# A gated mix of memory attention and a Fourier filter: fewer, larger numerator loads, split transposing loads, and a new order

## The chip, the core and the metric

One core of a Trainium2 chip runs the whole program. Its engines work side by side and in order, each through its own list of instructions: PE (TensorE, matrix products into PSUM), DVE (VectorE), ACT (ScalarE) and POOL (GpSimd) for elementwise work, and SP (SyncE), which here issues nearly all DMAs. PEld is the weight load of PE. The metric is the time of one execution on the device in microseconds, as the median of several runs.

## The reference

The input x has 2,048 tokens of 640 numbers. The result is a gate per token between two branches over the same x:

```python
g = sigmoid((x * gate_w).sum(-1, keepdims=True))
a = A(x, wq, wk, wv, wo, beta)
b = irfft2(rfft2(x) * (w_r + 1j * w_i))          # over tokens and channels
return g * a + (1 - g) * b
```

Branch A is attention in 4 segments of 512 tokens with 32 heads of 20 numbers. Inside a segment it is causal attention with softmax. Beside that, each head keeps a memory matrix M (20 x 20) and a sum z over all earlier segments:

```python
p = softmax(qs @ ks.T * scale + mask);  a_dot = p @ vs
a_mem = (phi(qs) @ M) / (phi(qs) @ z + 1e-6)
o = sigmoid(beta) * a_mem + (1 - sigmoid(beta)) * a_dot
M += phi(ks).T @ vs;  z += phi(ks).sum()
```

The o of all segments goes through wo. In segment 0 the memory is empty, so only a_dot counts.

## The kernel before

**Recording and replaying.** The program is not emitted in the order in which it is written. `record` (line 687 on) calls the parts one after another, and each operation is stored with what it reads and writes. `schedule` (line 104) then takes a list of numbers, PLAN (line 431 on), and emits in its order: a number divided by 16 is the operation, half of it modulo 8 is the engine, and its lowest bit picks for some PE products whether they run as one product of 128 columns or as four of 32. A second list gives the PSUM bank of each accumulation. So PLAN sets both the order on each engine and the choice of engine where there is one (`either`: DVE or POOL, `copy`: ACT or DVE). `emit` (line 140) puts in the waits that the dependences need. Nothing else decides the order; on each engine a late operation holds all behind it.

**Attention.** For a segment, `project` makes q, k and v from x, which transposing loads have turned. `attend` (line 1083 on) makes scores in PSUM, ACT exponentiates them (L1229, L1225), POOL or DVE set the masked part to zero (L1255, L1254), and `pv` multiplies with v. v carries a column of ones, so that each head's product has its numerators and, beside them, its denominator. The result is evicted (tile ub) and stored, tokens along the row, to a scratch tensor in HBM, u_scr: a segment has 1,024 rows of 512 tokens, 32 rows to a head, of which 20 are numerators and one the denominator.

**Denominators.** `denominators` loads the denominators of a segment back, takes reciprocals, multiplies by the gates and stores them to r_scr. From there each segment's r4 tile is loaded so that a partition holds the reciprocals of the head that it works for. Segment 3 has no time for that round trip: its reciprocals are built on PE (`pair_inverse`, `inverse_table`), for the first 24 heads (LATE) in r4, and for the last 8 heads separately (`late_group`, tile oL).

**Memory.** `mem_read_tile` (line 1032 on) multiplies phi(q) of 128 tokens with the masked memory matrix into two PSUM banks, computes the gated reciprocals of the denominators (tile dn), and one DVE product (name mem_mul, L1061 for segments 1 and 2, L1072 for segment 3) writes the quotients, tokens on the partitions, to the tile mem. The place of an element in a row of mem is chosen so that the row can be used turned: it is stored to HBM (o_scr; for segment 3 another scratch tensor with 6 x 128 columns), and later a transposing load brings it back as mT, channels on the partitions.

**Finishing.** `finish_tile` works on 128 tokens of a segment (a = 0 to 3). For a = 0 it loads the numerators of the whole segment as chunks of a tile oU: chunk c has 512 tokens in the row, and its partition (head, j) holds dimension 4c + j (segments 0 to 2: 5 chunks, 32 heads x 4) or 5c + j (segment 3: 4 chunks, 24 heads x 5). Each chunk is loaded alone (L1412, ld_u) and multiplied in place by r4 (L1414, normal). For a = 0 and 2 the memory part of 256 tokens is fetched by a transposing load (L1424, oT) into one of two mT buffers, with 5 or, in segment 3, 6 blocks of 128 channels. For each a, L1427 adds mT to oU (addmem); in segment 3, L1432 adds blocks 4 and 5 to oL (addlate). Then PE sums, in one PSUM bank per half row, the Fourier part (weights from the gate table) and the chunks times matching rows of wo (`late_weights` loads those, L772 and L777), and the row is evicted and stored.

The Fourier branch (`fft`) runs on the same engines beside the attention of all segments.

Of the kernel before, what the change touches and what calls it, by code (L numbers as in the profile page):

```python
# [8 lines left out]
ALU = mybir.AluOpType  # L9
# [3 lines left out]
P = 128  # L13
# [337 lines left out]
class Kern:  # L351
# [65 lines left out]
    def dma(self, dst, src, nbytes, r, w, tr=False, name="", after=(), queues=("sp",)):  # L417
# [1074 lines left out]
```

## Time and profile before

| what | value |
|---|---|
| time, median of 3 runs | 243.28 us (242.96 to 243.37) |
| the profiled execution | 241.93 us, its span 240.2 us |
| granted TensorE clock | 0.999 |
| PE busy | 220.6 us, 92% of the span |
| DVE busy | 209.2 us, 87% |
| ACT busy | 198.7 us, 83% |
| POOL busy | 134.2 us, 56% |
| DMA, mean | 183 GB/s |

The profile is of one execution. A row of a group of instructions names the line in the program, the engine, the operation, the tile written and the tiles read with their shapes, the number of instructions, then the busy time in us and the mean duration of one in ns, and at last the engine's idle time in front of them with what ended it. PE matrix products overlap, so a PE that is busy is not a PE at its peak. The tile mT shows under its own name, o_scr is the HBM tensor that it is loaded from, r is r4.

### The profile page before, as it was taken

The page shows a single profiled execution, that of the slowest core. Times are in us where ns is not written, and L with a number is a line of the kernel's source. Part 1 is how long each engine was busy: PE and PEld are TensorE (multiplying, and loading weights), DVE is VectorE, ACT ScalarE, POOL GpSimd, SP SyncE. Part 2 cuts the span into 40 slices and gives each one's busy share as a digit, 9 for nine tenths or more (in the row PEclk, how much of TensorE's full clock was granted, in tenths as well). Part 3 has the DMA queues.
Part 4 walks back from the last instruction along what each step waited for, and adds up shares of the span by engine and source line. Part 5 has one row for each costly group of instructions (what it writes and reads, how often), then busy time and mean ns, then how long its engine had stood idle before and what let it go on. Part 6 is the DMA issues. An engine that isn't in the chain of part 4 may idle for free.

```text
span 240.2 us, 9491 instructions
## 1 busy us (share of the span) xinstructions
PE 220.6 (92%) x4004; PEld 138.0 (57%) x4018; DVE 209.2 (87%) x476; ACT 198.7 (83%) x226; POOL 134.2 (56%) x205
## 2 busy tenths in 40 slices
PE   6989979999999889999998999999978999799994
PEld 2865546665654547555755457656544555466673
DVE  0889979999999899999999989899999996867752
ACT  2489879999999988988999799997989598589321
POOL 8613154547647594676659563694686606753100
PEclk9999999999999999999999999999999999999999
DMA  7999979989959764269769847565875899594323
GB/s 196 317 242 271 235 221 154 296 217 166 233 153 206 177 179 142 68 185 176 236 183 200 182 113 232 167 184 178 200 174 167 177 214 120 114 191 129 109 104 113
DMA packets 61897, 43.92 MB, mean 183 GB/s; under 512 B 31232, under 2 KB 58656, under 8 KB 61856
## 3 DMA queue, kind: packets, MB, share of 16 engines
q1 hardware_dynamic: 60816, 42.76, 76.0%
q8 instruction: 31, 0.51, 0.9%
q10 hardware_dynamic: 1040, 0.57, 0.8%
q14 instruction: 10, 0.08, 0.1%
HBM read 23.42 MB, written 13.87 MB: 155 GB/s over the span
## 4 chain that ended last, share of the span: by engine, by line
PE 43%; DVE 32%; ACT 8%; POOL 6%; issue 5%; DMA 3%; SPq 2%; DVEq 0%; POOLq 0%
PE psum L401 39%; ACT ex L1229 5%; POOL exc L1255 4%; DVE Pt L1346 4%; PE psum L399 4%; DVE G L1388 3%; DVE ub L408 2%; DVE Yt L1351 2%; DMA x<-in_A_x_dram 2%; DVE va L408 2%; SPq L423 2%; DVE Ac L408 2%; DVE mem L1072 2%; ACT exc L1225 2%; DVE Bt L408 1%
## 5 line engine op out<-in xcount | busy, mean ns | idle before, releaser
L1229 ACT ACTIVATE ex<-psum 128x2048 bf16<-128x2048 f32 x64 | 120.2, 1878 | 12.8 <-PE psum L401 12.1
L1255 POOL TENSOR_SCALAR_AFFINE_SELECT ex<-ex 128x256 bf16<-128x256 bf16 (+2 forms) x93 | 54.5, 593 | 49.7 <-ACT ex L1229 34.9
L1255 POOL TENSOR_SCALAR_AFFINE_SELECT exc<-exc 128x512 bf16<-128x512 bf16 (+3 forms) x23 | 29.1, 1271 | 10.4 <-DVE exc L1254 7.3
L401 PE MATMUL psum<-qkp 20*64 20x64 bf16 (+5 forms) x1024 | 31.1, 266 | 3.4 <-DMA qkp<-qk_scr 1.3
L401 PE MATMUL psum<-xT,wk 128*128 128x256 bf16 (+1 forms) x276 | 29.7, 273 | 0.5 <-issue 0.5
L401 PE MATMUL psum<-xT,wq 128*32 128x256 bf16 (+1 forms) x161 | 25.1, 326 | 1.2 <-issue 1.0
L1346 DVE TENSOR_TENSOR Pt<-psum,Wt 128x642 bf16<-128x642 f32 x32 | 25.7, 821 | 0.3 <-PE psum L401 0.2
L401 PE MATMUL psum<-wv,xT 128*32 128x320 bf16 (+3 forms) x387 | 24.5, 300 | 0.4 <-DVE Pt L1346 0.4
L401 PEld LDWEIGHTS psum<-qkp 20*64 20x64 bf16 (+1 forms) x1024 | 12.6, 100 | 19.1 <-ACT ex L1229 8.6
L401 PEld LDWEIGHTS psum<-xT,wk 128*128 128x128 bf16 (+1 forms) x276 | 19.9, 97 | 5.2 <-issue 2.0
L401 PE MATMUL psum<-ex,va 128*32 128x384 bf16 (+2 forms) x384 | 20.4, 320 | 1.9 <-POOL ex L1255 0.7
L401 PE MATMUL psum<-wo,oU 128*128 128x320 bf16 (+1 forms) x114 | 18.6, 300 | 0.0
L836 POOL TENSOR_TENSOR xsb<-xf 128x320 bf16<-128x320 bf16 (+2 forms) x12 | 9.0, 750 | 16.7 <-DVE xsb L836 13.7
L401 PEld LDWEIGHTS psum<-wv,xT 128*32 128x32 bf16 (+1 forms) x387 | 13.8, 96 | 6.4 <-issue 1.1
L408 DVE CAST ub<-psum 128x512 bf16<-128x512 f32 x23 | 15.7, 683 | 1.9 <-PE psum L401 1.4
L408 ACT ACTIVATE ot<-psum 128x320 bf16<-128x320 f32 x21 | 8.7, 440 | 10.5 <-PE psum L399 4.2
L1225 ACT ACTIVATE exc<-psum 128x1024 bf16<-128x1024 f32 (+1 forms) x12 | 15.7, 1308 | 1.8 <-PE psum L401 1.4
L1388 DVE TENSOR_TENSOR G<-eo,psum 128x320 bf16<-128x320 f32 x32 | 14.9, 481 | 1.8 <-ACT eo L408 1.4
L401 PE MATMUL psum<-big,Ac 128*128 128x161 bf16 (+2 forms) x93 | 14.2, 258 | 0.7 <-DVE mem L1061 0.3
L1254 DVE TENSOR_TENSOR ex<-ex,mk 128x256 bf16<-128x256 bf16 (+2 forms) x35 | 13.7, 397 | 1.0 <-ACT ex L1229 0.9
L401 PEld LDWEIGHTS psum<-xT,wq 128*128 128x128 bf16 (+1 forms) x175 | 10.4, 97 | 7.2 <-issue 0.7
L401 PEld LDWEIGHTS psum<-ex,va 128*32 128x32 bf16 x384 | 8.0, 95 | 11.2 <-issue 2.7
(145 smaller groups left out, 459.5 us busy)
## 6 DMA issues: line engine op xcount, KB each, us to landing
qkp<-qk_scr SPq DMA_DIRECT2D x28, 160.0 KB
tt<-tab_tt SPq DMA_DIRECT2D x8, 512.0 KB, 4.2
u_scr<-ub SPq DMA_DIRECT2D x15, 256.0 KB, 3.9
qk_scr<-qu SPq DMA_DIRECT2D x12, 256.0 KB, 2.1
xsb<-in_A_x_dram SPq DMA_DIRECT2D x8, 320.0 KB, 4.9
oU<-u_scr SPq DMA_DIRECT2D x15, 128.0 KB, 2.6
out_dram<-ot SPq DMA_DIRECT2D x12, 160.0 KB
Wt<-in_B_w_r_dram SPq DMA_DIRECT2D x16, 80.2 KB, 4.1
```

The source lines that it names most:

```text
L399: h = e.matmul(dst, wt, r_, start=st, stop=sp_, **{**kw, "tile_position": (0, q), "skip_group_check": True})
L401: h = e.matmul(o_, l_, r_, start=st, stop=sp_, **({**kw, "skip_group_check": True} if mode < 0 else kw))
L408: fns = {"act": lambda e: e.activation(dst(), src(), ACT.Copy), "dve": lambda e: e.tensor_copy(dst(), src())}
L423: return e.dma_start(d_, s_)
L836: self.either(lambda e, dst=dst, src=src, d0=d0, n=n, op=op: e.tensor_tensor(xs.ap(o + dst, [D, 2], [1, n]), xf.ap(src + d0, [321, 2], [1, ...
L1072: self.one("dve", lambda e, q0=q0, n=n, d0=d0, dst=dst, src=src, bc=bc: e.tensor_tensor(self.mem.ap(o + d0, *dst), self.ps(bank, q0 * VW, ...
L1225: self.one("act", lambda e, i=i: e.activation(self.exc.ap(self.exco(s, g + i), [192, 4], [768, m], [1, 128]), self.ps(bank, 128 * i, [512, ...
L1229: self.one("act", lambda e: e.activation(self.ex.ap(*d), self.ps(bank, *q), ACT.Exp, scale=SC), n, [bank], [self.exb(s, 2 * pr + gp, ks + ...
L1254: fns = {"dve": lambda e: e.tensor_tensor(av(d0), av(s0), mk(), ALU.min), "pool": lambda e: e.affine_select(ap(d0), ap(s0), [[0, 4 * m], [ ...
L1255: "pool": lambda e: e.affine_select(ap(d0), ap(s0), [[0, 4 * m], [step, n // 64], [1, 64]], ALU.is_ge, 0.0, base=base, channel_multiplier=-1)}
L1346: self.one("dve", lambda e, ri=ri, Pt=Pt, Wt=Wt, wo_=wo_, bank=bank: e.tensor_tensor(Pt.ap(ri * 322, [644, 2], [1, KD]), self.ps(bank, 0, ...
L1388: self.one("dve", lambda e, q=q, n2=n2, bank=bank, eo=eo: e.tensor_tensor(self.G.ap(n2 * D + 639 * q, [1 - 2 * q, 320]), eo.ap(q, [1, 320] ...
```

## The change

Four things change together.

1. The chunks of oU hold other dimensions: partition (head, j) of chunk c now has dimension 5j + c (segments 0 to 2) or 4j + c (segment 3). So neighbouring chunks of a partition are neighbouring rows of u_scr, and one descriptor can bring several. Chunks are loaded three and two at a time (segment 3: two and two), and each load is followed by one product over all its chunks, with r4 repeated. The loads of wo take the rows in the new order.
2. The memory products write the quotients to the places that the new chunks need. The number of elements and of instructions is the same; the loops over the chunks and over j change places, in the PSUM source and in the destination.
3. In segment 3 the transposing load of 6 blocks becomes two: blocks 4 and 5 first (with a dependence of its own, mL, which addlate waits for), and blocks 0 to 3 (mT, which addmem waits for).
4. PLAN is replaced as a whole: 2,223 operations instead of 2,243, with another order on every engine, other choices of engine and other PSUM banks. ACT issues the first load of wk, SP that of wq, which was the other way round.

```diff
-            self.dma(lambda c=c: self.wo[c].ap(0, [1, D]), lambda c=c: dap(self.wo_d, 4 * c * D, [DH * D, H], [D, 4], [1, D]),
+            self.dma(lambda c=c: self.wo[c].ap(0, [1, D]), lambda c=c: dap(self.wo_d, c * D, [DH * D, H], [5 * D, 4], [1, D]),
...
-            self.dma(lambda c=c: self.wo3[c].ap(0, [1, D], np_=5 * nh), lambda c=c: dap(self.wo_d, 5 * c * D, [DH * D, nh], [D, 5], [1, D]),
+            self.dma(lambda c=c: self.wo3[c].ap(0, [1, D], np_=5 * nh), lambda c=c: dap(self.wo_d, c * D, [DH * D, nh], [4 * D, 5], [1, D]),
...
             self.one("dve", lambda e: e.tensor_tensor(
-                self.mem.ap(i * D, [64, 2], [4, 16], [P, 5], [1, 4]), self.ps(bank, 0, [512, 2], [VW, 16], [4, 5], [1, 4]),
-                dn.ap(32, [16, 2], [1, 16], [0, 5], [0, 4]), ALU.mult), 640, [bank, rb], self.memb(s, i),
+                self.mem.ap(i * D, [64, 2], [4, 16], [1, 4], [P, 5]), self.ps(bank, 0, [512, 2], [VW, 16], [5, 4], [1, 5]),
+                dn.ap(32, [16, 2], [1, 16], [0, 4], [0, 5]), ALU.mult), 640, [bank, rb], self.memb(s, i),
...
-                (0, nh, 0, ([5 * nh, 2], [5, nh], [P, 4], [1, 5]), ([512, 2], [VW, nh], [5, 4], [1, 5]), ([0, DH],)),
+                (0, nh, 0, ([5 * nh, 2], [5, nh], [1, 5], [P, 4]), ([512, 2], [VW, nh], [4, 5], [1, 4]), ([0, DH],)),
...
-            for c in range(nc_):
-                home = (self.after_mid(("oU", c)) if s == 0 else [b("phq", t) for t in range(5)] if s == 1 else
+            for c0, n in ((0, 3), (3, 2)) if s < 3 else ((0, 2), (2, 2)):
+                home = (self.after_mid(("oU", c0)) if s == 0 else [b("phq", t) for t in range(5)] if s == 1 else
                         [b("va", 0, lt) for lt in range(4)] if s == 2 else [b("wqa"), b("wqb")])
-                self.dma(lambda c=c: oT.ap(c * L, [1, L], np_=np_), lambda c=c: dap(self.ud.ap(), (s * 1024 + nd * c) * L, [32 * L, nh], [L, nd], [1, L]),
-                         np_ * L * 2, [b("ud", s, i) for i in range(ng)], [ob[c]], name="ld_u", after=home)
-                self.either(lambda e, c=c: e.tensor_tensor(oT.ap(c * L, [1, L], np_=np_), oT.ap(c * L, [1, L], np_=np_),
-                                                           self.r4[s].ap(0, [1, L], np_=np_), ALU.mult), L, [b("r4", s)], [ob[c]], name="normal")
+                self.dma(lambda c0=c0, n=n: oT.ap(c0 * L, [1, n * L], np_=np_),
+                         lambda c0=c0, n=n: dap(self.ud.ap(), (s * 1024 + c0) * L, [32 * L, nh], [nc_ * L, nd], [1, n * L]),
+                         np_ * L * 2 * n, [b("ud", s, i) for i in range(ng)], ob[c0:c0 + n], name="ld_u", after=home)
+                self.either(lambda e, c0=c0, n=n: e.tensor_tensor(
+                    oT.ap(c0 * L, [L, n], [1, L], np_=np_), oT.ap(c0 * L, [L, n], [1, L], np_=np_), self.r4[s].ap(0, [0, n], [1, L], np_=np_), ALU.mult),
+                    n * L, [b("r4", s)], ob[c0:c0 + n], name="normal")
...
-                src = (lambda: dap(self.od.ap(), (s * L + a * P) * D, [D, 2 * P], [1, D])) if s < 3 else (
-                    lambda: dap(self.o3d.ap(), a * P * 6 * P, [6 * P, 2 * P], [1, 6 * P]))
-                self.dma(lambda mT=self.mT[k2]: mT.ap(0, [2 * P, n], [1, 2 * P]), src, 2 * P * P * n * 2,
-                         [b("od", s, i) for i in range(4)], [b("mT", k2)], tr=True, name="oT", after=self.after_mid(("mT", k2)))
+                src = (lambda k0: dap(self.od.ap(), (s * L + a * P) * D, [D, 2 * P], [1, D])) if s < 3 else (
+                    lambda k0: dap(self.o3d.ap(), a * P * 6 * P + k0 * P, [6 * P, 2 * P], [1, 2 * P + 2 * P * (k0 == 0)]))
+                for k0, m, key in ((0, 5, "mT"),) if s < 3 else ((4, 2, "mL"), (0, 4, "mT")):
+                    self.dma(lambda mT=self.mT[k2], k0=k0, m=m: mT.ap(k0 * 2 * P, [2 * P, m], [1, 2 * P]), lambda k0=k0: src(k0), 2 * P * P * m * 2,
+                             [b("od", s, i) for i in range(4)], [b(key, k2)], tr=True, name="oT", after=self.after_mid(("mT", k2)) + [b("mT", k2)])
...
-                                                                 mT.ap((4 + gl) * 2 * P + m0, [1, P]), ALU.add), P, [mb], [b("oL", gl, a)], name="addlate")
+                                                                 mT.ap((4 + gl) * 2 * P + m0, [1, P]), ALU.add), P, [b("mL", self.mtk[s])], [b("oL", gl, a)], name="addlate")
```

233 rows, old and new, of the table PLAN are left out of this document.

## The prediction, made before the changed kernel ran

> **What bounds the kernel now.** I read the page first (busy shares, the chain that ended last), then the busy times by stretch, then the waits of each stretch. The stretches: 76 to 146 us is the attention of segment 1, most of segment 2's and the middle of the Fourier branch; 146 to 184 the rest of segment 2 and the start of segment 3; 184 to 208 the last of the Fourier branch beside the first output tiles; 208 to 237 the output projections.
>
> ```profile
> PE 220.6 (92%) x4004; PEld 138.0 (57%) x4018; DVE 209.2 (87%) x476; ACT 198.7 (83%) x226; POOL 134.2 (56%) x205
> PE 43%; DVE 32%; ACT 8%; POOL 6%; issue 5%; DMA 3%; SPq 2%; DVEq 0%; POOLq 0%
> ```
> ```profile
> 76.00:146.00 70.00, 66.32 (x1174) 40.97 (x1180) 67.20 (x137) 64.74 (x63) 47.14 (x74) 1.00 0.70 169
> 146.00:184.00 38.00, 34.60 (x594) 21.13 (x593) 35.79 (x83) 34.28 (x38) 25.38 (x40) 1.00 0.68 189
> 184.00:208.00 24.00, 21.38 (x428) 12.43 (x428) 20.69 (x47) 19.19 (x24) 12.55 (x13) 1.00 0.83 151
> 208.00:237.00 29.00, 28.82 (x586) 19.14 (x586) 19.74 (x58) 16.21 (x23) 9.04 (x13) 1.00 0.59 134
> ```
> The columns are the stretch, its length, then busy time of PE, PEld, DVE, ACT and POOL, the granted clock (full speed here), the DMA share and GB/s. From 76 to 184 PE and DVE both work almost without a hole (PE idles 3.7 and 3.4 us, DVE 2.8 and 2.2), so more work on DVE there has little room. From 208 on PE never stops, DVE idles 9.3 us: the end comes when PE has done its matmuls, and it moves by what PE was held up before. The chain of waits from 171 to 179 us runs on DVE, through the memory read-out of the last segment:
>
> ```profile
> 171.61 0.72 DVE mem L1072
> 174.12 0.71 DVE mem L1072
> 176.92 0.71 DVE mem L1072
> 178.47 0.70 DVE mem L1072
> ```
> PE waits for just these products. The rows give total, times and longest; the first is from 76 to 146, the second from 146 to 184:
>
> ```profile
> PEld psum L401 <- DVE mem L1061: 1.8, 2, 1.2
> ...
> PEld psum L401 <- DVE mem L1072: 1.3, 3, 0.6
> ```
>
> **The change, part by part.** *Loads and normalisations of the numerators.* 19 loads become 8, 19 products become 8.
>
> ```profile
> L1414 DVE TENSOR_TENSOR oU<-oU,r 128x512 bf16<-128x512 bf16 x8 | 3.1, 413 | 0.0
> L1414 DVE TENSOR_TENSOR oU<-oU,r 120x512 bf16<-120x512 bf16 x3 | 1.1, 417 | 0.0
> L1414 POOL TENSOR_TENSOR oU<-oU,r 128x512 bf16<-128x512 bf16 x7 | 8.0, 1155 | 1.1 <-DMA r<-r_scr 0.7 <-DMA oU<-u_scr 0.4
> L1432 DVE TENSOR_TENSOR oL<-oL,mT 128x128 bf16<-128x128 bf16 x7 | 1.3, 219 | 0.0
> L1254 DVE TENSOR_TENSOR exc<-exc,mk 128x1024 bf16<-128x1024 bf16 x4 | 2.8, 690 | 0.7 <-POOL exc L1255 0.6
> ```
> On DVE (413 - 219) / 384 = 0.505 ns per element and 0.154 us fixed, so 1,024 elements take 0.67 us, which the mask product of that size (0.69, also with a repeated operand) confirms, and 1,536 take 0.93. The plan's numbers, decoded, put segment 0 on POOL and the other three on DVE: 2 x (0.93 + 0.67) + 2 x 0.67 = 4.5 us against 8 x 0.413 + 3 x 0.417 = 4.6. So DVE wins nothing here: it saves five fixed costs and takes over two products. POOL goes from 8 products (9.2 us) to two; by bounds of 1,155 ns per 512 elements (no fixed cost) these take at most 5.8, so it saves at least 3.4, on an engine that is 56% busy. I count that as nothing.
>
> The queue:
>
> ```profile
> L423 SPq DMA_DIRECT2D oU<-u_scr x19: 516/602/1560, 165.8 to 221.1; - x19
> DMA to landing us min/median/max: 2.5/2.6/3.2
> L421 SPq DMA_TRANSPOSE mT<-o_scr x6: 1342/1725/3625, 170.4 to 209.7; - x6
> DMA to landing us min/median/max: 7.3/7.7/8.1
> L421 SPq DMA_TRANSPOSE xT<-in_A_x_dram x9: 1241/1292/3195, 4.2 to 110.9; - x9
> ```
> SP issues 11 loads less (11 x 0.60 = 6.6 us) and two transposing loads more. A small transposing load (xT) still takes 1.29 us to issue, so the split costs 2.6 at that price, and the queue is 4.0 us lighter. What it would free is late next: after 184 us the transposes wait for their buffer and for landed data, not for the queue. A 384 KB load lands later than a 128 KB one (2.6); doubling that as an estimate, 2.6 us more, falls before products that wait on the reciprocals anyway. In the last segment the plan issues the split pairs where the two whole ones stood (206.9 and 209.7 us); both have landed by about 221 (209.7 + 3.6 + 8.1), and their first reader starts at 225.9. The four u loads that follow, at 218.3, become two, which gives back the 2.6. I take 0 for all DMA edits, bounds -1 and +1 us.
>
> *The memory products write another way.* This follows from the new row order (chunk c now holds dimensions 5j+c) and adds no instruction. Before, each product wrote runs of 4 or 5 neighbours; now consecutive elements lie 128 apart, 256 bytes.
>
> ```profile
> L1061 DVE TENSOR_TENSOR mem<-psum,dn 128x640 bf16<-128x640 f32 x8 | 6.6, 825 | 0.4
> L1072 DVE TENSOR_TENSOR mem<-psum,dn 128x480 bf16<-128x480 f32 x4 | 2.8, 706 | 0.1
> L1072 DVE TENSOR_TENSOR mem<-psum,dn 128x160 bf16<-128x160 f32 x4 | 1.3, 320 | 0.1
> L929 DVE COPY gT<-psum 8x128 f32<-8x128 f32 x4 | 1.5, 372 | 0.0
> L408 DVE COPY eo<-psum 128x321 f32<-128x321 f32 x4 | 1.9, 483 | 0.1
> ```
> No row shows a 256-byte step, so it is bounded. Lower end: runs of 4 cost nothing visible, since 160 elements take 320 and 640 take 825, or 1.05 ns per element throughout; +0. The other end: the gT copy is the one DVE instruction of this trace that writes every element away from its neighbour (32 bytes). Scaling the eo copy of the same type gives 483 - 193 x 1.05 = 280 ns for 128 elements; it takes 372, so 0.72 ns more per element. The 480 form supports it: 320 + 320 x 1.05 = 656 by the slope, 706 measured, where runs of 5 straddle. At 0.72 a 640 product takes 825 + 460 = 1.29 us; a 480 product 656 + 345 = 1.00, 0.30 more than now. 8 x 0.46 + 4 x 0.30 = +4.9 us of DVE. I take this end, since gT is nearest in kind (every write alone); both ends stay in the range. The Trainium skill (Advanced Engine Details and Errata, SBUF Cachelines) says that SBUF has 16-byte lines and that an access pattern which goes to a new line each time pays; the gT row (0.72 ns per element) agrees, and by a rule without price the sum would only be above the lower end.
>
> *The new order.* Decoded, the lists hold the same 1,082 PE operations; they reorder neighbours (no PE operation moves more than 21 places), and 201 changes of tile mode become 204. A weight load held by such a change shows as issue:
>
> ```profile
> PEld psum L401 <- issue: 6.2, 24, 0.5
> ```
> That is 0.26 us each, so 3 more cost 0 (hidden) to 0.8; I take 0.3. Between engines some work moves:
>
> ```profile
> L1254 DVE TENSOR_TENSOR ex<-ex,mk 128x256 bf16<-128x256 bf16 x20 | 7.2, 368 | 0.1
> L1254 DVE TENSOR_TENSOR exc<-exc,mk 128x512 bf16<-128x512 bf16 x8 | 4.0, 511 | 0.6 <-ACT exc L1225 0.6
> L408 DVE CAST Cp<-psum 128x512 bf16<-128x512 f32 x12 | 8.1, 682 | 0.2 <-PE psum L401 0.2
> L408 DVE CAST ot<-psum 128x320 bf16<-128x320 f32 x11 | 5.3, 485 | 5.7 <-PE psum L399 3.0 <-PE psum L401 2.6
> L836 DVE TENSOR_TENSOR xsb<-xf 128x320 bf16<-128x320 bf16 x9 | 2.8, 326 | 0.7 <-POOL xsb L836 0.7
> ```
> DVE gives 7 masks net to POOL (at 0.37 to 0.51, 2.6 to 3.6) and 3 late additions (0.22 each, 0.7). It takes 3 evictions net (0.49 to 0.68, 1.5 to 2.0, less the longer ones it gives away: about 1.1) and 3 folds and Fourier additions (0.33 each, 1.0). With the rows' lower ends that is -2.6 - 0.7 + 1.1 + 1.0 = -1.2. Summed along the decoded order, about 0.9 of it is gained by segment 2's last memory product (143 us) and 1.4 by 184 us. ACT saves 1.0 (three evictions net), POOL takes the masks into its idle time. At the start wq and wk change queues, with wq behind one x load; the key projections, which the new order puts first, cover it: 0, bounds -0.3 and +0.5.
>
> *Sum.* By 184 us DVE has 4.9 - 1.4 = 3.5 us more. It idled 5.0 us in these two stretches, and PE 7.1, so part goes into holes; but the places are those where PE already waits for mem, and the holes lie elsewhere. I take half, 1.7. With 0.3 for the mode changes: +2.0 us. The profiled execution took 241.93 us (span 240.2 and 1.7 around it), so 243.9; the median of the runs, 243.28, stands 1.35 above it, so 245.3.
>
> **The rivals.** *A: scattered writes are free.* Then DVE is 1.2 us lighter, ACT 1.0 and SP 4.0, and about 1.0 comes out at the end: 242.3, faster. For it: PSUM reads and short runs cost nothing; against it: the gT row. It decides where a 640 product stays below about 0.95 us (8 x 0.13 + 4 x 0.08 = 1.4, the relief by 184).
> *B: nothing hides it.* All 3.5 reach PE, with 0.3 and a late start of the output tiles: about 247.1. For it: DVE is 96% busy from 76 to 146; against: the 9.3 us that DVE idles behind 208, and the fact that tile work can swap in.
> *C: the two cancel*, 243.3.
> *D: the order also closes PE's largest hole.*
>
> ```profile
> DVE oU L1427 <- DMA mT<-o_scr: 1.1, 1, 1.1
> ...
> 208.03 0.34 PE L401 MATMUL psum<-fcat,omh 128*128 128x128 bf16 x3 [1.66 <-DVE ot L408]
> ```
> At 206 us an eviction comes late, since DVE waited for a transposed part and then ran two masks beside a long POOL product. The new list takes one of the masks off DVE there. With A this gives 242.3 - 1.5 = 240.8; alone it doesn't outweigh the writes. The same parts stand in the same sequence otherwise, so I give it little.
>
> **How the numbers follow.** Likeliest (half of the price arrives) 0.44; A 0.26; B 0.16; C 0.08; D 0.06. Predicted time 245.3 us, its own range 244.0 to 246.6. For eight in ten the range takes in A with its DMA bound and most of B: 241.5 to 247.2, leaving out D and the top of B. No change means within 0.2% (0.5 us), about what a measurement of this kernel can tell. Faster: A and D, 0.32; same: C, 0.08; slower: 0.60.
>
> **What would show it.** The 640 product of mem at 1.2 to 1.35 us, the 480 one near 1.0; DVE's sum 3 to 4 us up, ACT's and POOL's down; PE's busy time unchanged but more idle between 76 and 184 with DVE mem as the releaser; oU products of 0.67 and 0.93 us; SP with 241 issues. A is right if mem stays at 0.83. I am wrong in the absorbed half if PE's idle time does not grow although mem does, and wrong in the DMA part if oU or oL products wait for mT or u loads behind 215 us.

## The result, and the profile after

The changed kernel takes 268.06 us (median of 4 runs, 266.07 to 270.02). The kernel before, run beside it, takes 243.12. The ratio is 1.104, with a 95% interval of 1.099 to 1.110: it is a tenth slower, where the prediction had said 245.3 and a range up to 247.2. Some executions of a kernel take over 1.5% longer than its fastest, whatever the kernel; the times and ratios below leave these out. The profiled execution after took 267.85 us, its span 266.1.

The page of the changed kernel, first the busy times, then the granted clock in 40 slices of the span, then the shares of the chain that ended last:

```profile
PE 236.1 (89%) x4009; PEld 143.4 (54%) x4009; DVE 229.3 (86%) x467; ACT 199.2 (75%) x223; POOL 133.1 (50%) x206
...
PEclk9999999999999798999999597999955699999999
...
PE 48%; DVE 23%; DMA 13%; SPq 8%; issue 3%; ACT 3%; DVEq 0%
```

DVE works 20.1 us more than before (209.2), and PE 15.5 us more (220.6) for the same products. The PE's clock is no longer full: it has three dents, in slices 14 to 16, 23 to 25 and 30 to 32. The groups of instructions on DVE point to the cause. The first three rows answer to those of before (825, 706 and 320 ns), the last two are the larger normalisations:

```profile
L1060 DVE TENSOR_TENSOR mem<-psum,dn 128x640 bf16<-128x640 f32 x8 | 24.0, 2999 | 0.3
L1071 DVE TENSOR_TENSOR mem<-psum,dn 128x480 bf16<-128x480 f32 x4 | 9.2, 2292 | 0.1
L1071 DVE TENSOR_TENSOR mem<-psum,dn 128x160 bf16<-128x160 f32 x4 | 1.3, 321 | 0.1
L1414 DVE TENSOR_TENSOR oU<-oU,r 128x1536 bf16<-128x1536 bf16 x2 | 1.9, 950 | 0.0
L1414 DVE TENSOR_TENSOR oU<-oU,r 128x1024 bf16<-128x1024 bf16 x2 | 1.4, 684 | 0.0
```

A memory product now takes 3.0 us (segment 3: 2.29) in place of 0.8. That is 24.0 + 9.2 - 6.6 - 2.8 = 23.8 us more on DVE, in twelve instructions that compute what they computed before. The waits of the whole span (total, times, longest) show who stands behind them:

```profile
ACT ex L1228 <- PE psum L401: 21.2, 28, 2.9
...
PE psum L401 <- DVE mem L1060: 10.2, 6, 2.1
PEld psum L401 <- DVE mem L1060: 9.6, 5, 2.3
...
PEld psum L401 <- DVE mem L1071: 4.3, 3, 1.5
...
PE psum L401 <- DVE mem L1071: 3.2, 3, 1.2
```

PE waits for the products, and ACT for PE (before, ACT waited 12.1 us for PE ahead of `ex`; the rows of PE and PEld overlap and aren't to be added). The busy times by stretch show the three places where the products stand. Columns as in the prediction: the stretch, its length, busy time of PE, PEld, DVE, ACT, POOL, granted clock, DMA share, GB/s.

```profile
76.00:90.00 14.00, 9.95 (x167) 5.15 (x169) 13.82 (x21) 9.06 (x10) 6.96 (x10) 0.94 0.77 133
...
138.00:172.00 34.00, 26.26 (x394) 15.76 (x392) 29.72 (x51) 22.14 (x22) 13.28 (x25) 0.85 0.40 109
...
188.00:212.00 24.00, 19.13 (x286) 9.50 (x284) 22.36 (x41) 14.61 (x15) 11.55 (x18) 0.64 0.69 168
```

In the first and the third DVE is full and PE is not; in the third the clock falls to 0.64. The chain of waits runs through the third from product to product:

```profile
195.09 2.30 DVE mem L1071
...
199.30 2.31 DVE mem L1071
...
202.47 2.29 DVE mem L1071
```

### The profile page after: what moved, and what is told of

The parts are those of the page before. It is cut to its first block, busy times and chain, and to the rows that moved or that the text cites. A ratio compares the mean times of both kernels' runs of the same rounds, so it can differ in the third digit from the quotient of the medians.

```text
span 266.1 us, 9465 instructions
## 1 busy us (share of the span) xinstructions
PE 236.1 (89%) x4009; PEld 143.4 (54%) x4009; DVE 229.3 (86%) x467; ACT 199.2 (75%) x223; POOL 133.1 (50%) x206
## 4 chain that ended last, share of the span: by engine, by line
PE 48%; DVE 23%; DMA 13%; SPq 8%; issue 3%; ACT 3%; DVEq 0%
PE psum L401 43%; DVE mem L1060 7%; DMA qk_scr<-qu 5%; PE psum L399 5%; SPq L423 4%; SPq L421 4%; DVE mem L1071 3%; DMA pkn<-phk 3%; DVE Pt L1345 2%; DMA wk<-in_A_wk_dram 2%; DMA wv<-in_A_wv_dram 2%; ACT ex L1228 2%; DVE G L1387 2%; DVE phk L990 1%; DVE va L408 1%
## 5 line engine op out<-in xcount | busy, mean ns | idle before, releaser
L1228 ACT ACTIVATE ex<-psum 128x2048 bf16<-128x2048 f32 x64 | 120.2, 1878 | 21.7 <-PE psum L401 21.2
L1254 POOL TENSOR_SCALAR_AFFINE_SELECT ex<-ex 128x256 bf16<-128x256 bf16 (+2 forms) x99 | 58.6, 600 | 71.0 <-ACT ex L1228 47.2
L401 PE MATMUL psum<-qkp 20*64 20x64 bf16 (+5 forms) x1024 | 32.9, 277 | 2.3 <-DMA qkp<-qk_scr 1.3
L401 PE MATMUL psum<-xT,wk 128*128 128x256 bf16 (+1 forms) x276 | 32.1, 284 | 0.9 <-issue 0.4
L401 PE MATMUL psum<-xT,wq 128*128 128x512 bf16 (+1 forms) x175 | 30.2, 338 | 0.0
L401 PE MATMUL psum<-wv,xT 128*32 128x320 bf16 (+3 forms) x385 | 26.2, 308 | 0.6 <-DVE Bt L408 0.5
L401 PEld LDWEIGHTS psum<-xT,wk 128*128 128x128 bf16 (+1 forms) x276 | 20.9, 101 | 6.9 <-issue 2.1
L1060 DVE TENSOR_TENSOR mem<-psum,dn 128x640 bf16<-128x640 f32 x8 | 24.0, 2999 | 0.3
L401 PE MATMUL psum<-big,Ac 128*128 128x161 bf16 (+2 forms) x93 | 15.4, 265 | 2.6 <-DVE mem L1060 1.9
L408 DVE CAST ub<-psum 128x512 bf16<-128x512 f32 x23 | 15.8, 692 | 1.6 <-PE psum L401 1.2
L401 PE MATMUL psum<-big,Cp 128*128 128x321 bf16 (+1 forms) x74 | 16.4, 351 | 0.5 <-DVE eo L408 0.5
L401 PE MATMUL psum<-tt,Yt 128*128 128x256 bf16 (+1 forms) x92 | 15.5, 285 | 0.2 <-DVE qu L408 0.2
```

The source lines that it names most:

```text
L401: h = e.matmul(o_, l_, r_, start=st, stop=sp_, **({**kw, "skip_group_check": True} if mode < 0 else kw))
L408: fns = {"act": lambda e: e.activation(dst(), src(), ACT.Copy), "dve": lambda e: e.tensor_copy(dst(), src())}
L1060: self.one("dve", lambda e: e.tensor_tensor(self.mem.ap(i * D, [64, 2], [4, 16], [1, 4], [P, 5]), self.ps(bank, 0, [512, 2], [VW, 16], [5, ...
L1228: self.one("act", lambda e: e.activation(self.ex.ap(*d), self.ps(bank, *q), ACT.Exp, scale=SC), n, [bank], [self.exb(s, 2 * pr + gp, ks + ...
L1254: "pool": lambda e: e.affine_select(ap(d0), ap(s0), [[0, 4 * m], [step, n // 64], [1, 64]], ALU.is_ge, 0.0, base=base, channel_multiplier=-1)}
```

## The experiments

Two theories stood at the start. S: the scattered writes of the memory products (each element away from its neighbour) are the whole loss, and a write alone has a price per element that the prediction set too low. R: another part of the change (the order, the larger loads, the split transposes) has a share in it. When S held, two more questions came up: whether the length of the products is all that counts, or whether such writes also disturb other engines; and which part of the rest gains.

### The price of a scattered write by itself

The kernel e4_writes computes nothing of the reference (it writes zeros out); it runs DVE products of 640 elements with several destinations, each twice, and copies on DVE, ACT and POOL.

```diff
+ # runs of four (as before), 8 bytes each
+ e.tensor_tensor(room.ap(0, [4, 32], [P, 5], [1, 4]), src([20, 32], [4, 5], [1, 4]), ...)
+ # as in the change: neighbours 256 bytes apart
+ e.tensor_tensor(room.ap(0, [4, 32], [1, 4], [P, 5]), src([20, 32], [5, 4], [1, 5]), ...)
+ # steps of 4, 8, 16, ... 512 bytes; pairs; fp32; ACT and POOL
```

> A kernel of single instructions only (none of the reference is computed; it writes zeros): products of 640 elements whose destination differs in nothing but the place of the elements. Theory of distance (the price grows with the step between two writes): 16 to 32 bytes cost about the 0.7 ns per element of the gT copy, 256 bytes about 3.4 ns per element (2,170 ns more than 825), with values in between for 64 and 128 bytes. Theory of lines (each write that is alone pays the same): all steps from 16 or 32 bytes up cost the same, 2.2 us more. If the loop order of the source matters instead of the destination, the last two products (source with steps, destination dense) are slow too; I expect them at 825 ns. The copies on ACT and POOL show whether the price belongs to DVE alone; I expect ACT to pay as well.

The groups of that kernel: runs of four (L454), as in the change (L456), steps of 4, 8, 16 and 512 bytes (L460, L462, L464, L474), pairs of neighbours 128 bytes apart (L476), fp32 at 32 bytes (L480), ACT copying from PSUM, POOL and DVE copying from SBUF as in the change (L486, L487, L488), and a read of every fifth element with a dense write (L494):

```profile
L487 POOL COPY room<-sb 128x640 bf16<-128x640 bf16 x2 | 6.0, 3016 | 82.8 <-ACT room L486 82.8
L486 ACT ACTIVATE room<-psum 128x640 bf16<-128x640 f32 x2 | 6.0, 3004 | 75.9 <-DVE room L485 75.9
...
L474 DVE TENSOR_TENSOR room<-psum,small 128x640 bf16<-128x640 f32 x2 | 6.0, 3002 | 0.1
L456 DVE TENSOR_TENSOR room<-psum,small 128x640 bf16<-128x640 f32 x2 | 6.0, 2994 | 0.1
...
L464 DVE TENSOR_TENSOR room<-psum,small 128x640 bf16<-128x640 f32 x2 | 6.0, 2984 | 0.1
...
L488 DVE COPY room<-sb 128x640 bf16<-128x640 bf16 x2 | 3.2, 1586 | 12.3 <-POOL room L487 12.3
L462 DVE TENSOR_TENSOR room<-psum,small 128x640 bf16<-128x640 f32 x2 | 3.1, 1572 | 0.1
L480 DVE TENSOR_TENSOR roomf<-psum,small 128x640 f32<-128x640 f32 x2 | 2.6, 1301 | 0.1
...
L460 DVE TENSOR_TENSOR room<-psum,small 128x640 bf16<-128x640 f32 x2 | 1.7, 868 | 0.1
L476 DVE TENSOR_TENSOR room<-psum,small 128x640 bf16<-128x640 f32 x2 | 1.7, 826 | 0.1
L454 DVE TENSOR_TENSOR room<-psum,small 128x640 bf16<-128x640 f32 x2 | 1.6, 824 | 0.1
...
L494 DVE TENSOR_TENSOR room<-psum,small 128x640 bf16<-128x640 f32 x2 | 1.6, 824 | 0.1
```

The price is (2,994 - 824) / 640 = 3.4 ns per element. It is about the same from a step of 16 bytes (2,984) to 512 (3,002; the least in between is 2,826, at 32 bytes), so there distance doesn't matter. Nearer than that it does: at 8 bytes a product takes 1,572 ns, at 4 bytes 868, though each element is written alone there too. Two neighbours together cost nothing (826). The prediction's row, fp32 at a 32-byte step, repeats here: (1,301 - 824) / 640 = 0.75 ns, against 0.72 worked out from gT. So that row was read rightly; it was of the wrong type. Reading PSUM with a step of five elements, which the mended products below do, costs nothing (824). A DVE copy from SBUF pays less than the products from PSUM: 1,586 ns against 328 in runs of four, 2.0 ns per element (the same copy from PSUM takes 2,994).

### The writes alone, in the kernel before

```diff
-                self.mem.ap(i * D, [64, 2], [4, 16], [P, 5], [1, 4]), self.ps(bank, 0, [512, 2], [VW, 16], [4, 5], [1, 4]),
-                dn.ap(32, [16, 2], [1, 16], [0, 5], [0, 4]), ALU.mult), 640, ...
+                self.mem.ap(i * D, [64, 2], [4, 16], [1, 4], [P, 5]), self.ps(bank, 0, [512, 2], [VW, 16], [5, 4], [1, 5]),
+                dn.ap(32, [16, 2], [1, 16], [0, 4], [0, 5]), ALU.mult), 640, ...
```

Segment 3 likewise. The memory's channels then land in places where the old chunks don't look for them; nothing else differs from before.

> The kernel before, with its order, loads and rows, and only the loops of the two memory products taken from the changed kernel (so the memory part of the output has its channels in other places). If the scattered writes are the whole cause: DVE 23.7 us busier, mem products at 3.0 and 2.3 us, 262 to 270 us, with a clock below 0.95. If the new order or the loads carry a real share: clearly less, 250 to 258 us. If only half of DVE's price reached the end, as the prediction took: about 255 us.

It took 269.79 us (269.57 to 270.70), ratio 1.111 (1.104 to 1.117). Its products take 3,004 and 2,292 ns, again 23.8 us more on DVE, and the time grows by 26.8 us. The writes alone give the whole loss; the rest of the change isn't needed for it, against theory R.

### The rest of the change, with its writes mended

In e1_after_runs each chunk product of the changed kernel becomes two, one for each PSUM bank. Each needs one loop less, and its innermost loop writes runs of four or five again.

```diff
+                for q in range(2):
+                    h = e.tensor_tensor(
+                        self.mem.ap(i * D + 64 * q, [4, 16], [P, 5], [1, 4]), self.ps(bank, 512 * q, [VW, 16], [1, 5], [5, 4]),
+                        dn.ap(32 + 16 * q, [1, 16], [0, 5], [0, 4]), ALU.mult)
```

> The changed kernel, with each memory product of the chunks cut into two instructions, one per PSUM bank, whose destination has runs of 4 or 5 neighbours again (the same values at the same places). If the scattered writes are the whole cause: 242 to 244 us, products at about 0.5 us each, clock near 1.0. By the prediction's other terms: -1.0 from the lighter engines, +0.3 from mode changes, +0.15 us of DVE per product for the second instruction (12 x 0.15 = 1.8, half of it at the end): 243.5. If the rest of the change is bad as well: 247 or more.

In e5_after_pitch the heads of segments 1 and 2 stand 32 columns apart in PSUM, so that both banks fit in one regular step and one instruction writes all runs; segment 3 as in e1_after_runs.

```diff
+                self.mem.ap(i * D, [4, 32], [P, 5], [1, 4]), self.ps(bank, 0, [32, 32], [1, 5], [5, 4]),
+                dn.ap(32, [1, 32], [0, 5], [0, 4]), ALU.mult), 640, ...
```

> As the run before, but for segments 1 and 2 PE places a head's 22 columns 32 apart in PSUM, so that one instruction reads both banks and writes runs of 4 again (one product of 640 elements, about 825 ns if steps in the PSUM source are free). Expected 0.5 to 1 us less than the run before: 242 to 243.5 us. If PE pays for writing 22 columns at a pitch of 32, or DVE for reading every fifth element, it is not faster.

They took 239.53 us (ratio 0.985, 0.978 to 0.991) and 240.00 us (0.985, 0.978 to 0.992): both beat both kernels, and both came out below what was expected of them. The busy times and DVE's product rows of e5_after_pitch:

```profile
PE 222.0 (93%) x3995; PEld 138.1 (58%) x4009; DVE 207.1 (87%) x471; ACT 198.4 (83%) x223; POOL 132.4 (56%) x206
```
```profile
L1060 DVE TENSOR_TENSOR mem<-psum,dn 128x640 bf16<-128x640 f32 x8 | 6.6, 823 | 0.3
L1075 DVE TENSOR_TENSOR mem<-psum,dn 128x240 bf16<-128x240 f32 x8 | 3.0, 425 | 0.1
```

Its clock is 1.000 throughout. So the loss goes with the writes, and the rest of the change gains about 3 us; theory R falls. In what follows "mended" is this kernel.

### Does the length of the products explain all of it?

Three kernels start from the mended one. e9_scatter_seg3 takes the change's own products in segment 3 only. e8_long_dense and e10_long_dense32 keep the runs, and make the products long by cutting them into many small ones.

```diff
 # e9_scatter_seg3, segment 3
-                        self.mem.ap(o + 5 * nh * q, [5, nh], [P, 4], [1, 5]), ...   # two instructions
+                (0, nh, 0, ([5 * nh, 2], [5, nh], [1, 5], [P, 4]), ([512, 2], [VW, nh], [4, 5], [1, 4]), ...   # one
 # e8_long_dense (e10_long_dense32: for g in range(32), one head each)
+                for g in range(0, 32, 2):
+                    r = e.tensor_tensor(
+                        self.mem.ap(i * D + 4 * g, [4, 2], [P, 5], [1, 4]), self.ps(bank, 32 * g, [32, 2], [1, 5], [5, 4]),
+                        dn.ap(32 + g, [1, 2], [0, 5], [0, 4]), ALU.mult)
```

> The changed kernel with mended writes, its memory products cut into 16 (segment 3: 12) instructions of two heads each, 40 elements; they write runs of four and five, with the same values. An instruction of 32 elements from PSUM took 176 ns, so a product should take 2.8 to 3.1 us (2.1 to 2.4 us in segment 3), about as long as with lone writes. Theory that only the length on DVE matters: the same loss as in the changed kernel, 264 to 271 us, with the granted clock down to 0.93 to 0.95. Rival, that lone writes also disturb the other engines' use of SBUF: clearly less than that at the same length, 252 to 262 us.

> The changed kernel with mended writes in segments 1 and 2 and its own lone writes in segment 3 only: 4 products of 2.29 us in place of 4 of 0.85 us, 5.8 us more on DVE. Theory that DVE is the path there and nothing absorbs: 240.2 + 5.8 = 246 us, up to 248 with a lower granted clock. By the prediction's step that half of DVE's extra work arrives: 243.1 us. If segment 3 hides it all: 240.2 us.

> The changed kernel with mended writes, its memory products cut into 32 (segment 3: 24) instructions of one head each, 20 elements, in runs of four and five, with the same values. In e8_long_dense 16 instructions took 1.79 us of DVE per product (112 ns each), so this is to come near 3 us, the length of a product with lone writes. There DVE's 9.8 us more gave 10.1 us more. Theory that only the length on DVE counts: what DVE's groups grow by over e5_after_pitch, about 22 us, arrives whole, 260 to 268 us. Rival, that lone writes disturb other work beyond their length: under 256 us.

DVE's product rows in e8_long_dense, and then in e10_long_dense32:

```profile
L1062 DVE TENSOR_TENSOR mem<-psum,dn 128x40 bf16<-128x40 f32 x128 | 14.3, 191 | 0.3
L1080 DVE TENSOR_TENSOR mem<-psum,dn 128x40 bf16<-128x40 f32 x48 | 5.5, 198 | 0.1
```
```profile
L1062 DVE TENSOR_TENSOR mem<-psum,dn 128x20 bf16<-128x20 f32 x256 | 22.5, 165 | 0.3
L1080 DVE TENSOR_TENSOR mem<-psum,dn 128x20 bf16<-128x20 f32 x96 | 8.6, 170 | 0.1
```

In e8_long_dense the instructions overlap (14.3 us for 128), so a product came out at 1.8 us and not the 2.8 to 3.1 that I had expected; its time fell short of both ranges for that reason, and the finer cut was run. In the table DVE is the sum of the product rows without the 160-element ones, PE idle is the span less PE's busy time, and the loss is against the mended kernel's 240.00 us. Busy times and clocks are of the profiled executions. Each ratio is to the kernel before on the same chip.

| kernel | products, us of DVE | time, us | ratio to before (95%) | against mended | PE busy | PE idle | clock |
|---|---|---|---|---|---|---|---|
| mended | 9.6 | 240.00 | 0.985 (0.978 to 0.992) | | 222.0 | 16.2 | 1.000 |
| segment 3 scattered | 15.8 | 248.91 | 1.025 (1.017 to 1.033) | DVE +6.2, time +8.9 | 230.1 | 17.0 | 0.952 |
| long, dense, 16 | 19.8 | 250.35 | 1.033 (1.024 to 1.042) | DVE +10.2, time +10.4 | 225.9 | 23.1 | 0.978 |
| long, dense, 32 | 31.1 | 264.59 | 1.096 (1.088 to 1.104) | DVE +21.5, time +24.6 | 233.8 | 27.8 | 0.941 |
| the change | 33.2 | 268.06 | 1.104 (1.099 to 1.110) | DVE +23.6, time +28.1 | 236.1 | 30.0 | 0.935 |

With dense writes of nearly the same length the loss is nearly the same: 24.6 / 21.5 = 1.14 us per us of DVE, against 28.1 / 23.6 = 1.19. Each time has some 2 us of uncertainty, so the two agree. Within that, scattered writes hurt by their length alone, and the rival, that they disturb other engines, falls. (ACT's `ex` agrees: 1,878 ns in the changed kernel and in the one before.) Nothing is absorbed: 1.0 to 1.4 us arrive for each us on DVE, and e9_scatter_seg3 came out above the 246 to 248 us that were expected of it.

How more than all of it can arrive is seen in segment 3. The same 69 matrix products and then the same 192, first in e9_scatter_seg3, then in the mended kernel:

```profile
173.00:184.00 11.00, 6.99 (x69) 3.58 (x67) 10.69 (x15) 5.50 (x5) 8.24 (x9) 0.55 0.45 147
184.00:199.80 15.80, 15.66 (x192) 7.47 (x193) 11.24 (x25) 8.02 (x12) 5.13 (x5) 0.56 0.51 136
```
```profile
173.00:179.50 6.50, 4.96 (x69) 2.63 (x69) 6.22 (x19) 5.45 (x6) 5.56 (x5) 1.00 0.64 176
179.50:191.00 11.50, 10.22 (x192) 5.30 (x191) 10.95 (x25) 8.35 (x12) 7.84 (x10) 1.00 0.82 212
```

Ahead of 173 us and behind these stretches (47.3 and 47.2 us) the two kernels take the same time, so the whole loss lies here. While the scattered products run, e9_scatter_seg3 loses 4.5 us. It loses another 4.3 behind the last of them: PE hardly idles there (0.14 us), but it needs 15.66 us for what takes 10.22 in the mended kernel, since its clock stands at 0.56. The holes that the products leave on PE are followed by a slow clock, and about half of the loss is paid after the holes, through the clock. In the first half hole and clock can't be told apart, since no run has the holes at full clock.

### Which part of the rest gains

Four kernels take parts of the change, all with runs in the writes. In e6_order_alone everything but PLAN is as before; in e7_old_order everything is as in the mended kernel but PLAN follows the old order. e11_whole_tr and e12_sep_loads start from the mended kernel.

```diff
 # e11_whole_tr
-                for k0, m, key in ((0, 5, "mT"),) if s < 3 else ((4, 2, "mL"), (0, 4, "mT")):
+                for k0, m, key in ((0, 5, "mT"),) if s < 3 else ((0, 6, "mT"),):
 # e12_sep_loads
-            for c0, n in ((0, 3), (3, 2)) if s < 3 else ((0, 2), (2, 2)):
+            for c0, n in [(c, 1) for c in range(nc_)]:
```

> The kernel before with nothing of the change but its new order: five (four) separate loads and normalisations per segment stand one behind the other where the changed kernel has its two, the last memory part's whole transposing load stands where the changed kernel has the later of its two, and the PSUM banks are the changed kernel's. Memory products write runs of four as before. The prediction priced the order at -0.6 us at most by the end (DVE 1.2 us less in all, 0.3 us for more tile-mode switches), so by it 242 to 243.5 us. If the new order carries the 3 us that the changed kernel has gained with its writes mended, 239.5 to 241 us. If the merged loads carry them, 243 us or more, since their separate parts are then out of place.

> The changed kernel with mended writes (heads at a pitch of 32 in PSUM, as before in e5_after_pitch), but in the old order: each larger load stands where the last of its parts stood, each larger normalisation likewise, the split transposing loads one behind the other where the whole one stood. So this is the loads and normalisations alone. The prediction priced them at about nothing (DVE -0.1 us, POOL 3.4 us less off the path): 242.5 to 243.5 us. If they carry the gain of 3 us, 240 to 241 us. A loss, 244 us or more, if a larger load, which waits for the last of its parts, holds up the first additions.

> The changed kernel with mended writes, larger loads and normalisations, in the new order, but the last memory part in whole transposing loads, each standing where the changed kernel has the later of its two. The order alone left a hole of 3.1 us on PE between 190 and 200 us, which the mended kernel does not have. If the split of these loads is what fills it: 243 to 244 us, as with the order alone. If the larger loads and normalisations fill it: 239.5 to 241 us.

> The changed kernel with mended writes, split transposing loads and the new order, but with five (four) separate loads and normalisations per segment, one behind the other where the larger ones stood. If the split transposes are what fills the hole of the order alone: 239.5 to 241.5 us. If the larger loads do: 243 to 244 us. If both are needed, 241.5 to 243 us in this run and in e11_whole_tr alike.

| kernel | order | loads | transposes | time, us | ratio to before (95%) |
|---|---|---|---|---|---|
| e6_order_alone | new | separate | whole | 243.61 | 1.004 (1.000 to 1.008) |
| e12_sep_loads | new | separate | split | 243.05 | 1.004 (0.999 to 1.008) |
| e7_old_order | old | larger | split | 243.42 | 1.003 (0.999 to 1.007) |
| e11_whole_tr | new | larger | whole | 240.70 | 0.991 (0.987 to 0.995) |
| e5_after_pitch | new | larger | split | 240.00 | 0.985 (0.978 to 0.992) |

Neither the order nor the larger loads gain anything alone; together they gain. What the split of the transposes adds is not shown: the intervals of the last two rows overlap. That it is the split which closes the hole that the order alone leaves on PE is refuted: e12_sep_loads has it and gains nothing, e11_whole_tr lacks it and gains. DVE's normalisation rows of e12_sep_loads, then of e11_whole_tr:

```profile
L1307 DVE TENSOR_TENSOR oU<-oU,r 128x512 bf16<-128x512 bf16 x10 | 5.8, 632 | 1.5 <-DMA r<-r_scr 1.5
...
L1307 DVE TENSOR_TENSOR oU<-oU,r 120x512 bf16<-120x512 bf16 x4 | 1.5, 420 | 0.0
```
```profile
L1307 DVE TENSOR_TENSOR oU<-oU,r 128x1536 bf16<-128x1536 bf16 x2 | 1.9, 948 | 0.0
...
L1307 DVE TENSOR_TENSOR oU<-oU,r 120x1024 bf16<-120x1024 bf16 x2 | 1.4, 686 | 1.4 <-DMA oU<-u_scr 1.4
L1307 DVE TENSOR_TENSOR oU<-oU,r 128x1024 bf16<-128x1024 bf16 x2 | 1.4, 684 | 0.0
```

The new order puts three segments' normalisations on DVE. Separate, they cost 7.3 us there; larger, 4.7. But of these 2.6 us, 1.8 lie in one product of 2.26 us around 200 us, beside an addition on POOL (the median of the fourteen is 0.42); why it is that long was not shown. The queue has a part too. These rows are the issue of the last load of reciprocals (r), the DVE product that waits for it and PE's next wait, in e12_sep_loads; then the same issue in e11_whole_tr, where DVE doesn't wait for it:

```profile
193.59 0.55 SPq L423 DMA_DIRECT2D r<-r_scr  x1
198.02 0.76 DVE L1307 TENSOR_TENSOR oU<-oU,r 128x512 bf16<-128x512 bf16 x2 [1.47 <-DMA r<-r_scr]
199.24 0.72 PE L401 MATMUL psum<-G,fbg 128*32 128x320 bf16 x8 [1.11 <-DVE eo L408]
```
```profile
187.84 0.59 SPq L423 DMA_DIRECT2D r<-r_scr  x1
```

With separate loads SP issues six of them between 182.7 and 190.8 us, and r goes out 5.8 us later (the kernel was already 2.3 us behind at segment 3's first memory product, 172.5 against 170.2). DVE waits 1.5 us for it, and the copy `eo` that PE needs stands behind that product in DVE's list. So both DVE's time and the queue can be what makes the order and the larger loads go together; neither was taken out alone, and their shares stay open. From 190 to 210 us PE is busy 17.63 us with separate loads and 19.82 with larger ones (first e12_sep_loads, then e11_whole_tr):

```profile
190.00:210.00 20.00, 17.63 (x337) 10.01 (x335) 17.25 (x36) 14.69 (x17) 10.14 (x12) 1.00 0.66 146
```
```profile
190.00:210.00 20.00, 19.82 (x407) 12.17 (x393) 16.60 (x35) 17.43 (x17) 10.10 (x14) 1.00 0.63 129
```

What the old order lacks for the same gain was not tried further, nor were the larger loads with the old rows.

## Why the prediction was wrong, point by point

**What bounds the kernel** held. DVE and PE are both near full where the memory products stand, PE waits for just these, and the chain goes through them.

**The memory products' writes** is the step that failed. The effect was foreseen and its sign was right; the size was off by five. The prediction took the upper end "since gT is nearest in kind (every write alone)": 0.72 ns per element, +4.9 us. Measured: 3.4 ns, +23.8 us. gT writes 4-byte elements, the memory products 2-byte ones, and lone 2-byte writes cost 4.5 times as much (3.4 against 0.75 ns in e4_writes). The end that was called the other bound was no bound: no row of before had a lone 2-byte write, so nothing limited the price from above.

The Trainium skill (Advanced Engine Details and Errata, SBUF Cachelines) says that two accesses must hit a 16-byte line to absorb the memory's latency. That agrees with the free pairs (826 ns) and the lone writes from 16 bytes on (2,826 and more); at a step of 8 bytes, two elements to a line, it doesn't: 1,572 ns, where it would make 824.

**The absorbed half** failed too, as the second step. With the measured price, half would have given 0.5 x (23.8 - 1.4) + 0.3 = 11.5 us, or 254.8; all of it 22.7 us, or 266.0; measured 268.1. The argument from DVE's idle time (5.0 us in both stretches) found no room to speak of in the runs: in e8_long_dense 10.2 us of DVE gave 10.4 us. "PE's busy time unchanged" was wrong as well: it grew by 15.5 us while the clock fell to 0.935.

**Loads and normalisations.** The rows came out as worked out: 0.684 us for 1,024 elements (0.67 foreseen) and 0.950 for 1,536 (0.93). SP has 241 issues, as foreseen. The DMA edits taken as nothing are borne out alone (e7_old_order, 1.003), but not together with the order, where six loads on SP come ahead of r. The prediction had asked there whether the transposes wait for the queue, not whether r does.

**The new order** was priced by its sum, DVE 1.2 us less. Without the writes DVE is 2.3 us less busy in the mended kernel (207.1 - 209.2 - 0.2), and the time falls by 1.5%, where rival A let 1.0 us come out. The parts were costed one by one, and what they do together was missed: the gain is there only with the larger loads.

**The rivals.** A (free writes) has the wrong price, but shows what the change would be without them: 242.3 said, 240.0 measured. B (nothing hides it) was the nearest mechanism, at 247.1 on the wrong price, and still short of the slow clock; the likeliest case and C fall with the price. D gave 240.8 for A with PE's hole at 206 us closed. The mended kernel comes near that, and PE works 23.50 of the 24 us from 188 to 212:

```profile
188.00:212.00 24.00, 23.50 (x480) 14.13 (x482) 20.14 (x43) 19.49 (x21) 13.27 (x18) 1.00 0.79 141
```

That it is the mask moved off DVE that does it was not shown.

## What to carry to other kernels

When a change turns the loops of an instruction, look at what the innermost loop now does to the destination: a 2-byte element written without its neighbour made an instruction 3.6 times as long here, and turning the loops back, split by bank or with a regular pitch in the source, brought it back for next to nothing, since the stepped reads were free. A row bounds a price only where type and engine agree too; where no row has the kind of access at issue, the range has to stay open on that side. And an engine that is 96% busy beside another full one had no half to give here: count its extra time whole, and the slow clock that may follow PE's holes on top.

## What the runs showed of the hardware that was not expected

- A lone 2-byte write in DVE's products from PSUM cost 3.1 to 3.4 ns per element at steps of 16 to 512 bytes (2,826 to 3,002 ns for 640 elements against 824). In the order of the change, copies on ACT and POOL took as long as DVE's product: 3,004 and 3,016 ns against its 2,994, where runs of four take 704, 721 and 824. A DVE copy from SBUF took 1,586 against 328, in the same order. Lone 4-byte writes cost 0.75 ns at 32 bytes, pairs of 2-byte ones nothing. What makes a lone 2-byte write dear was not shown.
- PE's clock fell to half after short holes. Four stretches of 4 us of the changed kernel:

```profile
190.00:194.00 4.00, 2.75 (x49) 1.50 (x40) 3.90 (x8) 3.23 (x4) 0.37 (x1) 1.00 1.36 165
194.00:198.00 4.00, 2.69 (x20) 0.93 (x21) 3.93 (x7) 2.32 (x2) 4.00 (x4) 0.52 0.75 229
...
206.00:210.00 4.00, 4.00 (x43) 1.79 (x44) 3.95 (x8) 2.05 (x3) 0.00 (x0) 0.50 0.29 83
210.00:214.00 4.00, 3.67 (x76) 1.88 (x74) 2.27 (x6) 3.20 (x4) 1.91 (x2) 0.84 0.94 247
```

After 4 us with PE idle for 1.25 us, the clock stands at 0.5 from 194 to 210 us, and comes back after 4 us without a hole. Neither is a rule: from 154 to 158 us PE idled 1.79 us and the clock stayed full to 162, and in e9_scatter_seg3 it stood at 0.50 from 186 to 198 us with PE busy throughout. The Trainium skill (TensorE: Matmul & The Clock Gate, HAM oscillation — how this bites in real kernels) gives the rule that gaps above some 3.4 us throttle; here no wait of PE or its weight load is longer than 2.3 us, and the clock fell all the same, so the measurement decides.
